# Sliding-window attention feeding four gated experts: q and k loaded as 18 tokens per partition row and turned with an output stride of 18, batch 0 loaded first, masks from four selects

## The chip, the core and the metric

The kernel runs on one core of a Trainium2 chip. The metric is the device time of one execution in microseconds (us). The compute engines are PE (TensorE, matmuls and weight loads), DVE (VectorE), ACT (ScalarE) and POOL (GpSimd). SP only issues DMAs, and "SPq" and "ACTq" are the places in the traces where SP and ACT issue them. A time such as "67.9" without more is a moment of the profiled execution, counted from the start of its span.

## The reference

Eight batches of eight heads, 576 tokens, 64 elements per head. Each token attends to the tokens at most 32 away; the heads' results, put side by side, are the 512-wide input of a mixture of four attention experts, of which each token uses two.

```
scores = 0.125 * q @ k^T ;  scores = where(|i - j| <= 32, scores, -1e9)
x = softmax(scores) @ v                       # [8, 8, 576, 64] -> [8, 576, 512]
logits = x @ w_gate ;  w = softmax over the two largest of four
for e in range(4):
    a = causal softmax(0.125 * (x @ wq[e]) @ (x @ wk[e])^T)
    out += [e chosen] * w_e * (a @ (x @ wv[e])) @ wo[e]
```

## The kernel before

The work is cut by batch, and each batch passes through three stages. W (window scores) makes the masked exponentials AT of one batch; M makes the window result, the gate and the experts' scores of the batch before it; Z makes the experts' output of the batch before that. The stages N, W, M and Z of one pass i belong to batches i+1, i, i-1 and i-2. The text `ORDER` writes out the steps of one pass, and the loop runs it for i = 0 to 9. Inside `tc.manual_schedule()` every engine executes its instructions in exactly that written order, and so does SP with its DMAs: an instruction that waits holds up all later ones of its engine. What stands ahead of that block is ordered by a scheduler.

For each batch b and group g of four heads, `load_qk` brings q and k into tiles `qn` and `kn` of 128 partitions by 18 blocks by 64 elements: partition 32*h+p holds the tokens p, p+32, p+64, ..., so each piece in memory is one token's 64 floats, 256 bytes. Four DMAs, one per head, fill a tile. `turn` (L199) transposes a tile on DVE in 32 by 32 blocks into `Tkn` or `Tqn`, which have the 64 elements on partitions and the 576 tokens in order along the row; two instructions per tile. `win_scores` multiplies them on PE (L220), ACT takes the exponential (L226) and POOL multiplies it with the mask `MASK` (L227).

`load_v` reads v in 256-byte pieces (L89, L91) and then makes a second, shifted copy inside the on-chip memory with two DMAs (L93, L94), for which SP waits until v has landed. `win_av` (L255) needs both copies, and `win_sums` (L234), `win_norm` (L270, L272) follow. The two DVE waits that matter below are the turns of `kn`: in pass i, "W turn 1 kn" stands behind `win_norm` and ahead of the cast of the experts' keys (`QKE`, L347); "N turn 0 kn" stands ahead of the cast of the rest of the experts' values (`VE`, L368), whose end frees a PSUM slot for the next `win_scores`.

SP's order in a later pass is: three output stores (L448, L450), q and k of group 0 of the next batch, v of the next batch, the two copies, q and k of group 1. `load_weights` issues all weights from ACT's queue at the start, and DVE casts them to bf16 before its first turn. The masks are built on POOL: `MASK` from 18 selects over pieces of 96 to 160 columns, `SEL` (a 0/1 matrix that spreads a head's sums over 64 rows) from three selects over 2,048 columns.

Of the kernel before, what the change touches and what calls it, by code (L numbers as in the profile page):

```python
# [21 lines left out]
S = 576  # L22
HS = 288
# [3 lines left out]
def kernel(  # L27
# [23 lines left out]
        return min(128, S - 128 * t)  # L51

    consts = ctx.enter_context(tc.tile_pool(name="consts", bufs=1))
    natp = ctx.enter_context(tc.tile_pool(name="natp", bufs=3))
    qkt = ctx.enter_context(tc.tile_pool(name="qkt", bufs=2))
    vp = ctx.enter_context(tc.tile_pool(name="vp", bufs=2))
# [18 lines left out]
    vsb = {}  # L75

    def load_qk(b, g):
        for nm, src in (("qn", q), ("kn", k)):
            t = natp.tile([128, 18, 64], F32, name=nm, tag=nm)
            for hh in range(4):  # L80
                nc.sync.dma_start(t[32 * hh:32 * hh + 32, :, :],  # L81
                                  src[b, 4 * g + hh].rearrange("(tb p) d -> p tb d", p=32))
            nat[nm, b, g] = t

    def load_v(b):
# [9 lines left out]
        vsb[b] = t  # L95

    load_qk(0, 0)
    load_v(0)
    load_qk(0, 1)


    ident = consts.tile([128, 128], F32, name="ident")
    make_identity(nc, ident)
    ident_bf = consts.tile([128, 128], BF16, name="ident_bf")
    nc.vector.tensor_copy(ident_bf, ident)


    MASK = consts.tile([128, S], F32, name="MASK")
    nc.vector.memset(MASK, 1.0)
    for par in range(2):  # L110
        for m in range(5 - par):
            lo, hi = 128 * m - 32 + 64 * par, 128 * m + 96 + 64 * par
            if par == 1 and m == 0:
                lo = 0
            if par == 1 and m == 3:
                hi = S
            c0 = max(0, lo)
            c1 = min(S, hi)
            key0 = 128 * m + 64 * par
            ap = MASK[64 * par:64 * par + 64, c0:c1]  # L120
            nc.gpsimd.affine_select(ap, ap, pattern=[[1, c1 - c0]], compare_op=IS_GE, fill=0.0,
                                    base=c0 - key0 + 32, channel_multiplier=-1)
            nc.gpsimd.affine_select(ap, ap, pattern=[[-1, c1 - c0]], compare_op=IS_GE, fill=0.0,
                                    base=key0 + 32 - c0, channel_multiplier=1)

    OH = consts.tile([128, 8, 32], F32, name="OH")
    nc.vector.memset(OH, 0.0)
# [12 lines left out]
    nc.vector.tensor_reduce(NM, nmt, axis=AXX, op=ADD)  # L140

    SEL = consts.tile([128, 4, 4, 128], BF16, name="SEL")
    nc.vector.memset(SEL, 0.0)
    selv = SEL[:, :, :, :].rearrange("p j a (h d) -> p j (a h) d", d=64)
    for r in range(3):
        nc.gpsimd.affine_select(selv, selv, pattern=[[-32, 4], [-1, 8], [0, 64]], compare_op=NEQ,
                                fill=1.0, base=-8 * r, channel_multiplier=1)

    SELG = consts.tile([128, 4], F32, name="SELG")
    nc.vector.memset(SELG, 0.0)  # L150
# [10 lines left out]
    WV = consts.tile([128, NDT, 256], BF16, name="WV")  # L161
    WO = consts.tile([128, 2, DM], BF16, name="WO")

    def load_weights():
        nc.scalar.dma_start(WG[:, :, 0:4], moe_w_gate.rearrange("(t p) e -> p t e", p=128))
        for j in range(2):
            for n, src in enumerate((moe_wq, moe_wk)):
                if n == 0:
                    tmp = yp.tile([128, 2, NDT, 128], F32, name="tmpw", tag="ysb")
                for eo in range(2):  # L170
                    nc.scalar.dma_start(tmp[:, n, :, 64 * eo:64 * eo + 64],
                                        src[2 * j + eo].rearrange("(t p) d -> p t d", p=128))
                nc.vector.tensor_copy(WQK[j][n], tmp[:, n, :, :])
        tmpv = yp.tile([128, NDT, 256], F32, name="tmpv", tag="ysb")
        for e in range(E):
            nc.scalar.dma_start(tmpv[:, :, 64 * e:64 * e + 64],
                                moe_wv[e].rearrange("(t p) d -> p t d", p=128))
        nc.vector.tensor_copy(WV, tmpv)
        tmpo = yp.tile([128, 2, DM], F32, name="tmpo", tag="ysb")
        for e in range(E):  # L180
            nc.scalar.dma_start(tmpo[64 * (e % 2):64 * (e % 2) + 64, e // 2, :], moe_wo[e])
        nc.vector.tensor_copy(WO, tmpo)

# [9 lines left out]
    def turn(b, g, nm):  # L195
        T = qkt.tile([128, 2, S], F32, name="T" + nm, tag="T" + nm)
        n_ = nat.pop((nm, b, g))
        for dh in range(2):
            nc.vector.transpose(T[:, dh, :].rearrange("p (t x) -> p t x", x=32),  # L199
                                n_[:, :, 32 * dh:32 * dh + 32])  # L200
        qt_[b, g, nm] = T

    def win_scores(b, g, half):
        QT, KT = qt_[b, g, "qn"], qt_[b, g, "kn"]
        if half == 0:
            AT[b, g] = atp.tile([128, 4, S], F32, name="AT", tag="AT")
        A = AT[b, g]
        sl = [slot("sc0"), slot("sc1")]
        c0 = HS * half
        eb, ob = EBLK[half], OBLK[half]  # L210
        for s in range(3):
            for dh in range(2):
                for par, blk in ((0, eb), (1, ob)):
                    if s >= len(blk):
                        continue
                    m, lo, hi = blk[s]
                    k0 = 128 * m + 64 * par
                    for hh in range(4):
                        r = slice(32 * hh, 32 * hh + 32)
                        nc.tensor.matmul(  # L220
                            sl[hh // 2][64 * par:64 * par + 64, hh % 2, lo - c0:hi - c0],
                            KT[r, dh, k0:k0 + 64], QT[r, dh, lo:hi],
                            start=(dh == 0), stop=(dh == 1), skip_group_check=True)
        for p in range(2):
            ap = A[:, 2 * p:2 * p + 2, c0:c0 + HS]
            nc.scalar.activation(ap, sl[p][:, :, 0:HS], EXP, scale=scale_att)  # L226
            nc.gpsimd.tensor_tensor(out=ap, in0=ap,  # L227
                                    in1=MASK[:, None, c0:c0 + HS].to_broadcast([128, 2, HS]), op=MULT)

    def win_sums(b):  # L230
        ss = slot1("sums")
# [202 lines left out]
    def moe_y(b, t0):  # L434
# [14 lines left out]
        else:  # L449
            nc.sync.dma_start(out[b, 512:576, :], ysb[0:64, 0, :])  # L450


    load_weights()

    ORDER = """
        M win_av 0 | M win_av 1 | M win_sums | M win_av 2 | M win_av 3 | Z moe_av 1
        M win_norm 0 | M win_norm 1 | Z moe_turn 0 | M win_norm 2 | M win_norm 3 | Z moe_turn 1
# [62 lines left out]
```

## Time and profile before

| | |
|---|---|
| median of 3 runs | 387.86 us (380.88, 387.86, 388.38) |
| the profiled execution | 382.31 us, its span 380.6 us |
| mean granted TensorE clock in it | 0.929 of full speed |
| PE busy | 280.9 us (74% of the span) |
| DVE busy | 162.6 us (43%) |
| POOL busy | 151.8 us (40%) |
| ACT busy | 144.9 us (38%) |
| DMA packets | 129,351, of which 120,848 under 512 bytes |

The span is the time from the first to the last instruction. "Chain that ended last" is the work followed back from the last instruction, each step to what released it. "Waits" lists who stood idle and what ended it. The timeline gives start and length of each instruction or run of like instructions, and in brackets the idle time in front of it with its releaser. In the windows, the clock is the one granted to TensorE as a share of its full 2.4 GHz (0.50 is its lower level of 1.2 GHz).

### The profile page before, as it was taken

The numbers are of one execution on the slowest core, as the hardware profiler recorded it, in microseconds if no ns is written. First come the engines' busy times: TensorE is split into PE (matmuls) and PEld (weight loads), VectorE is DVE, ScalarE is ACT, GpSimd is POOL, SyncE is SP. The second block draws the span as 40 slices with busy tenths as digits, with TensorE's granted clock in tenths as the row PEclk, the third lists the DMA queues.
The fourth block names the chain that finished last, engine by engine and source line by source line (L and its number), as shares of the span: only waits on it lengthen the run. The fifth ranks groups of instructions, "written<-read, shape, count | busy, mean of one in ns | idle before, by whom it ended". The sixth has DMA issues, their size and how long they took to land.

```text
span 380.6 us, 12750 instructions
## 1 busy us (share of the span) xinstructions
PE 280.9 (74%) x5680; PEld 207.7 (55%) x5680; DVE 162.6 (43%) x375; ACT 144.9 (38%) x217; POOL 151.8 (40%) x208
## 2 busy tenths in 40 slices
PE   0050686688897889869885879678978998798864
PEld 0040574457655665648564765566556856583641
DVE  4420441553726262444644282527443355343341
ACT  0120223254163615543363326361635245623432
POOL 8732336244252714443534425271436154612110
PEclk9999999689898996999899999999996989996986
DMA  9999969979089943969097918875597812002103
GB/s 164 201 158 184 183 137 174 171 153 122 2 198 178 159 67 117 185 143 157 14 231 156 180 23 199 178 152 76 165 186 143 107 49 79 3 4 87 39 0 124
DMA packets 129351, 48.02 MB, mean 126 GB/s; under 512 B 120848, under 2 KB 120848, under 8 KB 129296
## 3 DMA queue, kind: packets, MB, share of 16 engines
q1 hardware_dynamic: 122112, 45.10, 65.9%
q10 hardware_dynamic: 7184, 2.11, 3.4%
q8 instruction: 44, 0.72, 0.8%
q14 instruction: 11, 0.09, 0.1%
HBM read 30.42 MB, written 9.44 MB: 105 GB/s over the span
## 4 chain that ended last, share of the span: by engine, by line
PE 45%; DMA 14%; SPq 14%; DVE 11%; ACT 9%; issue 4%; ACTq 1%; POOL 0%; DVEq 0%; POOLq 0%
SPq L81 11%; PE sc L220 10%; PE u L255 10%; DMA kn<-in_k_dram 9%; PE po L408 7%; PE py L441 5%; ACT ATE L385 5%; PE sums L234 4%; DVE XTF L272 3%; PE pp L340 3%; ACT AT L226 2%; DVE Tkn L199 2%; PE pv L362 2%; PE ps L382 2%; DVE OE L417 2%
## 5 line engine op out<-in xcount | busy, mean ns | idle before, releaser
L227 POOL TENSOR_TENSOR AT<-AT,MASK 128x576 f32<-128x576 f32 x64 | 88.6, 1406 | 101.1 <-ACT AT L226 101.1
L220 PE MATMUL sc<-Tqn,Tkn 32*64 32x128 f32 (+3 forms) x2560 | 62.0, 311 | 56.6 <-DVE Tqn L199 35.4
L220 PEld LDWEIGHTS sc<-Tqn,Tkn 32*64 32x64 f32 x2560 | 52.0, 156 | 67.6 <-DVE Tqn L199 22.6
L226 ACT ACTIVATE AT<-sc 128x576 f32<-128x576 f32 x64 | 38.2, 648 | 120.1 <-PE sc L220 120.1
L385 ACT ACTIVATE ATE<-ps 128x1024 bf16<-128x1024 f32 x64 | 50.8, 835 | 27.7 <-PE ps L382 27.6
L274 POOL CAST XTB<-XTF 128x576 bf16<-128x576 f32 x32 | 21.3, 666 | 72.8 <-DVE XTF L272 72.8
L255 PE MATMUL u<-AT,vsb 128*64 128x64 f32 (+1 forms) x1024 | 39.0, 235 | 7.5 <-ACT ATE L385 6.8
L199 DVE STREAM_TRANSPOSE Tkn<-kn 128x576 f32<-128x576 f32 x32 | 22.9, 751 | 47.5 <-DMA kn<-in_k_dram 47.5
L255 PEld LDWEIGHTS u<-AT,vsb 128*64 128x64 f32 x1024 | 35.5, 142 | 10.7 <-ACT ATE L385 7.6
L259 ACT COPY us<-u 128x576 f32<-128x576 f32 x32 | 20.4, 638 | 39.3 <-PE u L255 39.3
L382 PE MATMUL ps<-QKE 64*128 64x512 bf16 (+2 forms) x192 | 22.7, 294 | 13.4 <-ACT AT L226 6.8
L389 POOL TENSOR_SCALAR_AFFINE_SELECT ATE<-ATE 128x384 bf16<-128x384 bf16 x32 | 15.9, 521 | 40.8 <-ACT ATE L385 40.8
L347 DVE CAST QKE<-pp 128x576 bf16<-128x576 f32 x16 | 12.0, 747 | 47.1 <-PE pp L340 47.1
L408 PE MATMUL po<-VE,ATE 128*128 128x65 bf16 (+2 forms) x480 | 27.9, 201 | 2.0 <-POOL ATE L389 1.6
L408 PEld LDWEIGHTS <-ATE 128*128 128x128 bf16 (+2 forms) x480 | 22.1, 103 | 8.1 <-POOL ATE L389 1.7
L415 DVE RECIPROCAL po<-po 128x8 f32<-128x8 f32 (+1 forms) x32 | 6.2, 194 | 47.1 <-PE po L408 46.5
L446 ACT COPY ysb<-py 128x1024 f32<-128x1024 f32 (+1 forms) x24 | 19.5, 880 | 17.6 <-PE py L441 9.2
L441 PE MATMUL py<-WO,OTT 128*128 128x512 bf16 (+1 forms) x80 | 25.3, 463 | 1.2 <-DVE OTT L432 1.1
L199 DVE STREAM_TRANSPOSE Tqn<-qn 128x576 f32<-128x576 f32 x32 | 22.8, 750 | 0.0
L272 DVE TENSOR_TENSOR XTF<-us,rb 128x576 f32<-128x576 f32 x32 | 22.3, 737 | 0.6 <-PE rb L270 0.6
L239 DVE RECIPROCAL sums<-sums 128x144 f32<-128x144 f32 x8 | 8.5, 1067 | 32.6 <-PE sums L234 32.6
L362 PE MATMUL pv<-WV,XTB 128*128 128x256 bf16 (+1 forms) x160 | 21.9, 289 | 0.0
(67 smaller groups left out, 317.3 us busy)
## 6 DMA issues: line engine op xcount, KB each, us to landing
qn<-in_q_dram SPq DMA_DIRECT2D x64, 144.0 KB, 5.3
kn<-in_k_dram SPq DMA_DIRECT2D x64, 144.0 KB, 5.3
vsb<-in_v_dram SPq DMA_DIRECT2D x32, 256.0 KB, 5.6
out_dram<-ysb SPq DMA_DIRECT2D x16, 512.0 KB, 2.9
vsb<-vsb SPq DMA_DIRECT2D x8, 512.0 KB, 5.1
vsb<-vsb SPq DMA_DIRECT2D x8, 384.0 KB, 7.6
vsb<-in_v_dram SPq DMA_DIRECT2D x8, 128.0 KB, 4.4
out_dram<-ysb SPq DMA_DIRECT2D x8, 128.0 KB, 3.4
```

The source lines that it names most:

```text
L81: nc.sync.dma_start(t[32 * hh:32 * hh + 32, :, :], src[b, 4 * g + hh].rearrange("(tb p) d -> p tb d", p=32))
L199: nc.vector.transpose(T[:, dh, :].rearrange("p (t x) -> p t x", x=32), n_[:, :, 32 * dh:32 * dh + 32])
L220: nc.tensor.matmul(sl[hh // 2][64 * par:64 * par + 64, hh % 2, lo - c0:hi - c0], KT[r, dh, k0:k0 + 64], QT[r, dh, lo:hi], start=(dh == 0), ...
L226: nc.scalar.activation(ap, sl[p][:, :, 0:HS], EXP, scale=scale_att)
L227: nc.gpsimd.tensor_tensor(out=ap, in0=ap, in1=MASK[:, None, c0:c0 + HS].to_broadcast([128, 2, HS]), op=MULT)
L255: nc.tensor.matmul(u[64 * x:64 * x + 64, half, lo - HS * half:hi - HS * half], V[:, c, h, :], A[:, h % 4, lo:hi], start=True, stop=True, s ...
L272: nc.vector.tensor_tensor(out=XTF[:, pair, :].rearrange("p (a c) -> p a c", c=HS), in0=st.pop(("us", b, pair)), in1=rb[:, :, 0:HS], op=MULT)
L362: nc.tensor.matmul(o, XTB[:, dt, 128 * t:128 * t + n], WV[:, dt, :], start=(dt == 0), stop=(dt == NDT - 1))
L382: nc.tensor.matmul(ps[0:rows, eo, at:at + hi - lo], QKE[r, 1, 128 * kt:128 * kt + nrow(kt)], QKE[r, 0, lo:hi], start=True, stop=True)
L385: nc.scalar.activation(ATE[0:rows, :, 512 * c:512 * c + w], ps[0:rows, :, 0:w], EXP, scale=scale_moe)
L408: nc.tensor.matmul(po[0:n, eo, 65 * qt:65 * qt + 65], ATE[0:nk, eo, o:o + n], VE[0:nk, kt, 2 * j + eo, :], start=(kt == 0), stop=(kt == qt))
L441: nc.tensor.matmul(py[0:n, t - t0, :], OTT[:, j, 128 * t:128 * t + n], WO[:, j, :], start=(j == 0), stop=(j == 1))
```

## The change

q and k tiles are loaded by one DMA each, in which partition 32*h+p holds the 18 consecutive tokens 18*p to 18*p+17: one piece of 4,608 bytes per partition. The tokens then lie across the blocks, and `turn` writes each block's 32 columns 18 floats apart to put them in order again. k is loaded before q. At the start both groups of batch 0 are loaded before its v; group 0 of batch 1 follows, then the weights, now from SP's queue and behind the copies of v. All four turns of batch 0 are done first; those of batch 1's group 0 stand ahead of the sums of batch 0. The weights' casts go from DVE at the start to ACT in pass 1. The window mask is built from four selects over 512 or 640 columns, `SEL` from three selects over 32 columns and one spreading copy on DVE. For batch 0 the masks are multiplied on DVE. One dummy exponential loads ACT's table early.

```diff
 def load_qk(b, g):
-        for nm, src in (("qn", q), ("kn", k)):
+        for nm, src in (("kn", k), ("qn", q)):
             t = natp.tile([128, 18, 64], F32, name=nm, tag=nm)
-            for hh in range(4):
-                nc.sync.dma_start(t[32 * hh:32 * hh + 32, :, :],
-                                  src[b, 4 * g + hh].rearrange("(tb p) d -> p tb d", p=32))
+            nc.sync.dma_start(t[:, :, :].rearrange("p s d -> p (s d)"),
+                              src[b, 4 * g:4 * g + 4].rearrange("h (p s) d -> (h p) (s d)", s=18))
...
     load_qk(0, 0)
+    load_qk(0, 1)
     load_v(0)
-    load_qk(0, 1)
...
+    MASKP = consts.tile([128, 640], F32, name="MASKP")
...
+        nc.gpsimd.affine_select(ap, ap, pattern=[[0, nb], [1, 128]], compare_op=IS_GE, fill=0.0,
+                                base=0, channel_multiplier=-1)
+        nc.gpsimd.affine_select(ap, ap, pattern=[[0, nb], [-1, 128]], compare_op=IS_GE, fill=0.0,
+                                base=64, channel_multiplier=1)
+    MASK = MASKP[:, 32:608]
...
+    def spread_sel(_):
+        nc.vector.tensor_copy(SEL[:, :, :, :].rearrange("p j a (h d) -> p (j a h) d", d=64),
+                              sels[:, :, :].rearrange("p j h -> p (j h)")[:, :, None].to_broadcast([128, 32, 64]))
...
-    def load_weights():
-        nc.scalar.dma_start(WG[:, :, 0:4], moe_w_gate.rearrange("(t p) e -> p t e", p=128))
+    def load_weights(_):
+        nc.sync.dma_start(WG[:, :, 0:4], moe_w_gate.rearrange("(t p) e -> p t e", p=128))
...
+    def cast_weights(_):
+        for j in range(2):
+            for n in range(2):
+                nc.scalar.copy(WQK[j][n], wtmp[j][:, n, :, :])
+        nc.scalar.copy(WV, wtmp["v"])
+        nc.scalar.copy(WO, wtmp["o"])
...
 def turn(b, g, nm):
         for dh in range(2):
-            nc.vector.transpose(T[:, dh, :].rearrange("p (t x) -> p t x", x=32),
+            nc.vector.transpose(T[:, dh, :].rearrange("p (t s) -> p s t", s=18),
                                 n_[:, :, 32 * dh:32 * dh + 32])
...
 def win_scores(b, g, half):
-            nc.gpsimd.tensor_tensor(out=ap, in0=ap,
-                                    in1=MASK[:, None, c0:c0 + HS].to_broadcast([128, 2, HS]), op=MULT)
+            eng = nc.vector if b == 0 else nc.gpsimd
+            eng.tensor_tensor(out=ap, in0=ap,
+                              in1=MASK[:, None, c0:c0 + HS].to_broadcast([128, 2, HS]), op=MULT)
...
+    early = {("turn", 0), ("turn", 1), ("load_qk", 1)}
     with tc.manual_schedule():
+        load_qk(1, 0)
+        load_weights(0)
         turn(0, 0, "kn")
         turn(0, 0, "qn")
+        turn(0, 1, "kn")
+        turn(0, 1, "qn")
+        spread_sel(0)
         for i in range(B + 2):
...
+                if i == 0 and (fn, b) in early and not (fn == "load_qk" and args == ["1"]):
+                    continue
+                if i == 1 and fn == "win_sums":
+                    turn(1, 0, "kn")
+                    turn(1, 0, "qn")
+                if fn == "win_norm" and i == 1 and args == ["0"]:
+                    cast_weights(0)
```

The order of SP's DMAs from the start up to the group 1 of batch 1 was this. The number in a tile's name tells two tiles apart: `kn_99` and `kn_117` are groups 0 and 1 of batch 0, `kn_307` and `kn_427` those of batch 1; the weights are not on this queue.

```order
L81 DMA qn_94<-in_q_dram 32x18x64 x4
L81 DMA kn_99<-in_k_dram 32x18x64 x4
L89 DMA vsb_104<-in_v_dram 128x8x64 x4
L91 DMA vsb_104<-in_v_dram 64x8x64
L93 DMA vsb_104<-vsb_104 64x4x512
L94 DMA vsb_104<-vsb_104 64x3x512
L81 DMA kn_117<-in_k_dram 32x18x64 x4
L81 DMA kn_307<-in_k_dram 32x18x64 x4
L89 DMA vsb_312<-in_v_dram 128x8x64 x4
L93 DMA vsb_312<-vsb_312 64x4x512
L81 DMA kn_427<-in_k_dram 32x18x64 x4
```

Of the changed kernel the same stretch reads as follows; here `kn_97` and `kn_101` are batch 0, `kn_201` and `kn_387` batch 1.

```order
L82 DMA kn_97<-in_k_dram 128x1152
L82 DMA kn_101<-in_k_dram 128x1152
L90 DMA vsb_105<-in_v_dram 128x8x64 x4
L82 DMA kn_201<-in_k_dram 128x1152
L94 DMA vsb_105<-vsb_105 64x4x512
L82 DMA qn_203<-in_q_dram 128x1152
L175 DMA tmpw_206<-in_moe_wq_dram 128x4x64 x2
L179 DMA tmpv_216<-in_moe_wv_dram 128x4x64 x4
L183 DMA tmpo_221<-in_moe_wo_dram 64x512 x4
L90 DMA vsb_286<-in_v_dram 128x8x64 x4
L94 DMA vsb_286<-vsb_286 64x4x512
L82 DMA kn_387<-in_k_dram 128x1152
```

Batch 0's second group now stands ahead of its v, and 17 weight DMAs stand between the first copies and batch 1's v; group 1 of batch 1 is still behind batch 1's copies.

On DVE the start, from the first turn to the end of the window's normalising in pass 1, has these turns in the kernel before (`Tkn_369` is batch 1's group 0, `Tkn_625` its group 1):

```order
L173 CAST WQ1_213<-tmpw_225 128x512
L178 CAST WV_215<-tmpv_232 128x1024
L199 STREAM_TRANSPOSE Tkn_246<-kn_99 128x576 x2
L199 STREAM_TRANSPOSE Tkn_252<-kn_117 128x576 x2
L199 STREAM_TRANSPOSE Tkn_369<-kn_307 128x576 x2
L239 RECIPROCAL sums_516<-sums_516 128x144
L272 TENSOR_TENSOR XTF_595<-us_495,rb_597 128x576
L199 STREAM_TRANSPOSE Tkn_625<-kn_427 128x576 x2
L347 CAST QKE_703<-pp_714 128x576
```

and these in the changed one:

```order
L207 STREAM_TRANSPOSE Tkn_226<-kn_97 128x18x32 x2
L207 STREAM_TRANSPOSE Tqn_235<-qn_103 128x18x32 x2
L148 COPY SEL_163<-sels_164 128x2048
L236 TENSOR_TENSOR AT_239<-AT_239,MASKP_122 128x2x288 x4
L236 TENSOR_TENSOR AT_340<-AT_340,MASKP_122 128x2x288 x4
L207 STREAM_TRANSPOSE Tkn_475<-kn_201 128x18x32 x2
L248 RECIPROCAL sums_481<-sums_481 128x144
L281 TENSOR_TENSOR XTF_566<-us_454,rb_568 128x576
L207 STREAM_TRANSPOSE Tkn_596<-kn_387 128x18x32 x2
L356 CAST QKE_668<-pp_679 128x576
```

The casts of the weights have gone, eight mask multiplications have come, and the turn of batch 1's group 1 still stands ahead of the cast of the experts' keys.

## Rows read from the trace of the kernel before

**Rows 1.** The page: span, and the chain that ended last, by line
```profile
span 380.6 us, 12750 instructions
...
SPq L81 11%; PE sc L220 10%; PE u L255 10%; DMA kn<-in_k_dram 9%; PE po L408 7%; PE py L441 5%; ACT ATE L385 5%; PE sums L234 4%; DVE XTF L272 3%; PE pp L340 3%; ACT AT L226 2%; DVE Tkn L199 2%; PE pv L362 2%; PE ps L382 2%; DVE OE L417 2%
```

**Rows 2.** The page's DMA queues and issues: size of each, median us to landing
```profile
q10 hardware_dynamic: 7184, 2.11, 3.4%
...
kn<-in_k_dram SPq DMA_DIRECT2D x64, 144.0 KB, 5.3
...
vsb<-vsb SPq DMA_DIRECT2D x8, 384.0 KB, 7.6
```

**Rows 3.** Waits of 0 to 88.8 us: who waited, total us, times, longest us
```profile
DVE Tkn L199 <- DMA kn<-in_k_dram: 32.5, 4, 16.1
...
PE ps L382 <- DVE QKE L347: 4.9, 1, 4.9
```

**Rows 4.** Waits of 88.8 to 294.7 us, the five batches with loads
```profile
DVE Tkn L199 <- DMA kn<-in_k_dram: 15.0, 5, 3.5
...
PE sc L220 <- DVE VE L368: 11.5, 5, 2.8
```

**Rows 5.** Timeline 0 to 75 us: start, length, engine, what, idle before it
```profile
22.03 2.74 PE L220 MATMUL sc<-Tqn,Tkn 32*64 32x96 f32 x84 [22.03 <-DVE Tqn L199]
...
46.36 4.18 PE L255 MATMUL u<-AT,vsb 128*64 128x96 f32 x64
...
57.99 1.34 PE L220 MATMUL sc<-Tqn,Tkn 32*64 32x96 f32 x73 [0.28 <-DVE XTF L272]
...
63.72 1.39 PE L220 MATMUL sc<-Tqn,Tkn 32*64 32x64 f32 x80
...
67.89 1.44 DVE L199 STREAM_TRANSPOSE Tkn<-kn 128x576 f32<-128x576 f32 x2 [9.29 <-DMA kn<-in_k_dram]
...
70.02 0.61 PE L382 MATMUL ps<-QKE 64*128 64x512 bf16 x2 [4.91 <-DVE QKE L347]
```

**Rows 6.** Timeline 130 to 173 us, one batch of the steady part
```profile
156.82 1.23 DVE L365 CAST VE<-pv 128x1024 bf16<-128x1024 f32 x1 [2.18 <-PE pv L362]
...
159.51 0.18 DVE L317 SCALAR_TENSOR_TENSOR pl<-MSK,pl 128x20 f32<-128x20 f32 x1
...
161.81 0.38 PE L220 MATMUL sc<-Tqn,Tkn 32*64 32x96 f32 x4
...
162.36 1.44 DVE L199 STREAM_TRANSPOSE Tkn<-kn 128x576 f32<-128x576 f32 x2 [2.67 <-DMA kn<-in_k_dram]
...
164.16 1.37 PE L220 MATMUL sc<-Tqn,Tkn 32*64 32x96 f32 x76 [1.97 <-DVE VE L368]
```

**Rows 7.** Windows: us, busy per engine (count), PE clock, DMA share, GB/s
```profile
0.00:2.00 2.00, 0.00 (x0) 0.00 (x0) 0.85 (x3) 0.00 (x0) 1.11 (x8) 1.00 0.04 10
0.00:20.00 20.00, 0.00 (x0) 0.00 (x0) 8.09 (x16) 1.28 (x1) 15.70 (x40) 1.00 1.18 184
36.00:38.00 2.00, 0.00 (x0) 0.00 (x0) 0.00 (x0) 0.00 (x0) 0.00 (x0) 1.00 1.41 169
108.00:110.00 2.00, 2.00 (x47) 1.49 (x49) 0.30 (x1) 1.00 (x2) 0.00 (x0) 1.00 1.02 367
```

**Rows 8.** Groups by line and shape on DVE: busy us, mean ns of one
```profile
L199 DVE STREAM_TRANSPOSE Tkn<-kn 128x576 f32<-128x576 f32 x32 | 22.9, 751 | 47.5 <-DMA kn<-in_k_dram 47.5
...
L272 DVE TENSOR_TENSOR XTF<-us,rb 128x576 f32<-128x576 f32 x32 | 22.3, 737 | 0.6 <-PE rb L270 0.6
...
L328 DVE TENSOR_TENSOR G<-pl,ssum 128x20 f32<-128x20 f32 x8 | 1.6, 194 | 0.3
...
L309 DVE TENSOR_TENSOR GE<-pl,m 128x20 f32<-128x20 f32 x8 | 1.4, 178 | 0.3
```

**Rows 9.** Groups by line and shape on ACT
```profile
L446 ACT COPY ysb<-py 128x1024 f32<-128x1024 f32 x16 | 15.8, 1025 | 17.6 <-PE py L441 9.2 <-issue 7.7 <-ACT AT L226 0.6
L345 ACT CAST QKE<-pp 128x576 bf16<-128x576 f32 x16 | 10.2, 638 | 13.0 <-issue 7.8 <-PE pp L340 5.2
```

More of the change, by code (lines that the diff above doesn't have):

```diff
@@ L53 @@
     consts = ctx.enter_context(tc.tile_pool(name="consts", bufs=1))
+    stage = ctx.enter_context(tc.tile_pool(name="stage", bufs=1))
     natp = ctx.enter_context(tc.tile_pool(name="natp", bufs=3))
@@ L97 @@
     load_qk(0, 0)
+    load_qk(0, 1)
     load_v(0)
-    load_qk(0, 1)
     ident = consts.tile([128, 128], F32, name="ident")
     make_identity(nc, ident)
+    warm = consts.tile([128, 1], F32, name="warm")
+    nc.scalar.activation(warm, ident[:, 0:1], EXP)
     ident_bf = consts.tile([128, 128], BF16, name="ident_bf")
     nc.vector.tensor_copy(ident_bf, ident)
[L108 to L124, printed above, removed]
+    MASKP = consts.tile([128, 640], F32, name="MASKP")
+    nc.vector.memset(MASKP[0:64, :], 1.0)
+    nc.vector.memset(MASKP[64:128, :], 0.0)
+    nc.vector.memset(MASKP[64:128, 64:576], 1.0)
+    for p0, ap in ((0, MASKP[0:64, :]), (64, MASKP[64:128, 64:576])):
+        ap = ap.rearrange("p (m c) -> p m c", c=128)
+        nb = 5 if p0 == 0 else 4
+        nc.gpsimd.affine_select(ap, ap, pattern=[[0, nb], [1, 128]], compare_op=IS_GE, fill=0.0,
[3 more added lines that the diff above has]
+    MASK = MASKP[:, 32:608]
     OH = consts.tile([128, 8, 32], F32, name="OH")
@@ L142 @@
     SEL = consts.tile([128, 4, 4, 128], BF16, name="SEL")
-    nc.vector.memset(SEL, 0.0)
-    selv = SEL[:, :, :, :].rearrange("p j a (h d) -> p j (a h) d", d=64)
+    sels = consts.tile([128, 4, 8], BF16, name="sels")
+    nc.vector.memset(sels, 0.0)
     for r in range(3):
-        nc.gpsimd.affine_select(selv, selv, pattern=[[-32, 4], [-1, 8], [0, 64]], compare_op=NEQ,
-                                fill=1.0, base=-8 * r, channel_multiplier=1)
+        nc.gpsimd.affine_select(sels, sels, pattern=[[-32, 4], [-1, 8]], compare_op=NEQ, fill=1.0,
+                                base=-8 * r, channel_multiplier=1)
+    def spread_sel(_):
+        nc.vector.tensor_copy(SEL[:, :, :, :].rearrange("p j a (h d) -> p (j a h) d", d=64),
+                              sels[:, :, :].rearrange("p j h -> p (j h)")[:, :, None].to_broadcast([128, 32, 64]))
     SELG = consts.tile([128, 4], F32, name="SELG")
@@ L450, in moe_y @@
             nc.sync.dma_start(out[b, 512:576, :], ysb[0:64, 0, :])
-    load_weights()
     ORDER = """
```

21 lines of the change are left out of this document (9 added, 12 removed).

## Prediction

> **What bounds the kernel now.** I read the chain that ended last first. No engine fills it: its largest entry by line is SP issuing q and k (SPq L81, 11% of a span of 380.6 us), and another 9% is the landing of `kn` [rows 1]. The waits then tell where the lateness costs something. Up to 88.8 us DVE stands idle 32.5 us in four waits for `kn`, the longest 16.1; the last of them stops PE for 4.9 us, because the cast of the experts' keys stands behind the turn [rows 3]. In the five later batches that have loads, DVE waits 15.0 us for `kn` and PE loses 11.5 us of it behind the `VE` cast [rows 4]. So the loads of q and k cost time twice: once in the start-up, once a little in each batch. The reader is to see in the timeline that PE had nothing else to do: in one batch the turn starts at 162.36 after 2.67 us of idling, and PE, done with its few ready matmuls at 161.81 + 0.38 = 162.19, goes on only at 164.16 [rows 6].
>
> **The later batches.** There the stores go first on SP, then q and k of the next batch. Eight issues become two, and 256-byte pieces become 4,608-byte ones. A tile is four DMAs of 144.0 KB, 590 kB [rows 2]. In 256-byte pieces q and k move at 169 GB/s, and the two-microsecond window in which output stores of 2 KB rows dominate shows 367 GB/s [rows 7]. The trace has no piece of 4,608 bytes, so the price of a tile lies between 590/367 = 1.6 us and 590/169 = 3.5 us; I take 2.0 us (about 300 GB/s), near the row it is most like. At either end `kn` lands well before DVE asks, since seven issues ahead of it fall away as well. DVE is then free at 159.51 + 0.18 = 159.69; the two transposes (1.44) and the small `VE` cast (about 0.4) end at 161.5, ahead of PE's 162.19. All 11.5 us of PE's waits would go, were the transposes unchanged.
>
> **The strided write.** The transposes now write each run of 32 elements 72 bytes apart. No transpose in the trace writes with a stride. What bounds it: 751 ns for 576 elements is about one element per cycle of 1.04 ns plus 0.15 us, which is the lower end (+0). The nearest row with a strided write is `G`, 20 elements written 20 bytes apart: 194 ns, against 178 ns for `GE`, the same count written in order [rows 8], so 0.8 ns per element. For 576 elements that is +0.46 us; rounding up to one whole extra cycle gives +0.6 us, which I take, since 20 elements are a thin sample. The Trainium skill (SBUF — State Buffer, section "Door 1: The DMA port swizzle") speaks against the change here: accesses need at least two hits on a 16-byte line for full bandwidth, and each crossing to a new line pays; it gives no size for DVE. The `G` row agrees in direction. Without any penalty the sum below would be 4 us lower; its harsh reading is a rival.
>
> At +1.2 us per turn, most turns have cover: the turn of `qn` in pass i ends 2.18 us before DVE is needed for the large `VE` cast [rows 6]. The turn at 159.69 then ends the `VE` cast at 162.7, 0.5 us after PE's 162.19, so five batches lose 5 x 0.5 = 2.5 us plus a little semaphore time. Gain of the later batches: 11.5 - 2.8 = **8.7 us**.
>
> **The start-up.** What PE waits for at 67.89 is `kn` of batch 1, group 1 [rows 5]. I follow SP's new order up to it. Transfers begin at about 2.0 (the first two microseconds move 10 GB/s) [rows 7]. Four tiles of batch 0 at 2.0: 10.0. Then v, 4 x 256 + 128 KB = 1.18 MB, still in 256-byte pieces at 169 GB/s, 7.0 us: 17.0, known to SP at about 17.7. `kn` of batch 1 runs meanwhile. The copies of v take 7.6 us from issue [rows 2]: 25.3. `qn` of batch 1: 27.3. The weights are 2.11 MB [rows 2]: 0.52 MB of 2 KB rows at 367 and 1.58 MB at 169, 10.8 us: 38.1. v of batch 1, 7.0 us: 45.1, known at 45.8. Its copies: 53.4. `kn` of group 1 behind them, 2.0: **55.4**, where it was 67.89: 12.5 us earlier. Its own strided turn takes 1.2 back and stands directly ahead of the cast that PE waits for: 11.3 us. Bounds: at 1.6 us a tile, and with the copies not holding up `kn`, it lands at about 51; at 3.5 us a tile at about 64.
>
> What else the edit moves must be done before that. `win_av` of batch 0 starts when the copies land, 25.3 instead of 46.36 [rows 5]. Its scores need `qn` (6.7, with its turn 9.4) and four times 2.74 us [rows 5], about 21 with the exponentials. The masks on DVE: four turns end near 13.4, the spreading copy of 2,048 columns costs 2.6 us at the pace of `XTF` (737 ns for 576), and eight products at 737 ns end near 22; the copies of v cover that up to 25.3. The mask selects on POOL (15.70 us busy of the first 20 [rows 7]) are shorter and needed at 16, so I put them at nothing. From `win_av` to the first scores of batch 1 took 57.99 - 46.36 = 11.6 us: 36.9. The casts now in ACT's way cost four times 638 ns and twice 1025 ns [rows 9], 4.6 us: 41.5, later than the weights' landing. From there to the point where PE has nothing left took 65.11 - 57.99 = 7.1 us [rows 5]: 48.6. So the casts lie under the wait for `kn` with 7 us to spare, and without that wait they would cost their 4.6 us.
>
> **The sum.** 382.31 us for the profiled execution (its span 380.6 and 1.7 around it), less 11.3 at the start, less 8.7 in the later batches: 362.3, so **362 us**. The median of the three runs is 387.86, 1.5% above the profiled one, and the lowest is 380.88; if the changed kernel scatters alike, its median may lie up to 5 us above the sum, which the range takes in.
>
> **Rivals.**
> *Strided writes are dear (the other side).* At c cycles per element a transpose costs 0.15 + 0.6c us. At c = 4 (2.55 us) `kn` of group 1 is turned 3.6 us later than unstrided; in each batch the `qn` turn eats its 2.18 us of slack and 1.4 us more, and the turn at 159.69, itself 1.4 later, ends the cast at about 166.6 instead of 164.1: 2.5 us lost in each of five batches, 1.5 in the sixth. 382.3 - 12.5 + 3.6 + 14 = 387, no change; at c = 5 the same working gives about 400. It becomes slower by 2% (390) from about 4.3 cycles. The `G` row, under two cycles, speaks against it. The Trainium skill's rule on lines (SBUF — State Buffer, the same section) leaves the size open. The turns would read 2.5 us and more each. Slower 0.04, unchanged 0.05.
> *The loads do not speed up per byte* (3.5 us a tile). `kn` lands at 64, 3.5 us earlier, 1.2 of it lost in the turn; the later batches still gain 8.7, since seven fewer issues and one tile ahead instead of two are enough. 371 us. The 367 GB/s row speaks against it. 0.11.
> *`kn` of group 1 comes before PE needs it*, because weights and copies overlap better than my queue in single file. Then 48.6 is the floor: 70.02 - 48.6 = 21.4 instead of 11.3, and the sum is 352. For it: DMA shares above 1 in the windows mean that transfers overlap [rows 7]; against it: SP still waits for v before issuing the copies, and `kn` is behind them. 0.18.
> *Another wait takes the place in the later batches*, for example the keys' or the values' cast further back on DVE, and only the start-up gains: 371 us. Against it: PE's other waits on DVE do not hang on the loads. 0.10.
>
> **How the numbers follow.** My forecast has 0.52, with 355 to 369 as its own range. The cases with 371 and 352 add 0.39, and the overall range of 350 to 376 takes them in, with their scatter. About 2% is what a measurement of this kernel can tell from no change. Faster by over 2% needs less than about 375 on the profiled scale, which the forecast and three rivals give: 0.91 by the cases, cut to 0.86 for a cost that I have not seen; within 2%: 0.09; slower: 0.05.
>
> **What would show it.** Right: transposes of about 1.35 us; DVE's waits for `kn` after the start gone, and PE's wait behind the `VE` cast under 1 us per batch; the last wait for `kn` ending near 55, with PE stopped before it; `win_av` of batch 0 near 25. Wrong: transposes above 2.5 us; `kn` still awaited in each batch; or `win_av` of batch 0 not starting before 35, which would mean that v or its copies are later than the sum has them.

## The result, and the profile after

The median is 349.82 us (347.33 to 353.33) against 386.77 for the kernel before beside it: ratio 0.910, 95% interval 0.895 to 0.925. The forecast was 362 with a range of 350 to 376, so the direction was right, and the time lies 0.2 us below the range: the gain was larger than forecast. The profiled execution took 351.94 us, 30.4 less than the 382.31 before, where 20.0 were forecast. Medians here and below are over all executions, while ratios and intervals leave out those in a slower state at a lower granted clock; of the kernel before, 27 executions beside the experiments took 375.86 to 392.84 us at mean clocks of 0.958 to 0.897.

The page of the kernel after, span and chain that ended last, by engine and by line:

```profile
span 350.2 us, 12556 instructions
...
PE 62%; DVE 15%; ACT 9%; DMA 5%; SPq 4%; issue 3%; ACTq 0%; POOL 0%; POOLq 0%; DVEq 0%
PE sc L228 13%; PE u L264 9%; PE pp L349 8%; PE po L417 7%; PE py L450 7%; ACT ATE L394 5%; PE pv L371 5%; PE sums L243 4%; DVE XTF L281 4%; ACT AT L234 4%; DVE Tkn L207 3%; DMA kn<-in_k_dram 3%; PE pl L308 3%; PE ps L391 3%; PE pg L299 2%
```

SP's issuing of q and k, the largest entry before at 11% [rows 1], is gone from the list; the landing of `kn` fell from 9% to 3%, and PE now fills 62% of the chain.

I cut both profiles at the first `win_av` of pass 2 (88.80 before, 73.16 after) and at that of pass 7 (294.65 and 261.69). Timeline of the kernel after, the places of [rows 5]:

```profile
23.01 3.79 PE L264 MATMUL u<-AT,vsb 128*64 128x64 f32 x60 [1.84 <-DMA vsb<-vsb]
...
49.83 2.34 DVE L207 STREAM_TRANSPOSE Tkn<-kn 128x576 f32<-128x576 f32 x2 [14.65 <-DMA kn<-in_k_dram]
...
52.80 0.61 PE L391 MATMUL ps<-QKE 64*128 64x512 bf16 x2 [12.37 <-DVE QKE L356]
...
73.16 2.06 PE L264 MATMUL u<-AT,vsb 128*64 128x96 f32 x58 [0.97 <-ACT ATE L394]
```

The last awaited `kn` is turned at 49.83 instead of 67.89, PE goes on at 52.80 instead of 70.02, and pass 2 begins **15.6 us** earlier. The waits of 73.2 to 261.7 us, the five later batches (us in total, times, longest):

```profile
DVE VE L374 <- PE pv L371: 4.7, 5, 0.9
...
PE pp L349 <- ACT ATE L394: 2.1, 5, 0.4
PE ps L391 <- ACT AT L234: 2.0, 5, 0.4
PE pv L371 <- ACT AT L234: 2.0, 5, 0.4
...
PEld sc L228 <- DVE VE L377: 1.2, 5, 0.2
```

DVE's 15.0 us for `kn` and PE's 11.5 behind `VE` [rows 4] are no longer among them. Windows of the same five batches, first before, then after; the columns are the length, busy time (instructions) of PE, weight loads, DVE, ACT and POOL, then PE clock, DMA share and GB/s:

```profile
88.80:294.65 205.85, 169.53 (x3551) 126.58 (x3551) 96.48 (x226) 89.37 (x136) 85.39 (x106) 0.94 0.74 137
```

```profile
73.16:261.69 188.53, 163.50 (x3546) 123.55 (x3551) 113.22 (x226) 89.01 (x136) 85.34 (x106) 0.97 0.54 146
```

They are **17.3 us** shorter. PE's work is the same, but it was busy 6.0 us less, at a mean clock of 0.97 instead of 0.94. What follows pass 7 took 88.5 instead of 85.95 us, **2.6** more. The sum, -15.6 - 17.3 + 2.6, is -30.3.

The turns and the other new work of DVE (groups by line and shape: busy us, mean ns of one):

```profile
L207 DVE STREAM_TRANSPOSE Tkn<-kn 128x576 f32<-128x576 f32 x32 | 37.3, 1240 | 15.4 <-DMA kn<-in_k_dram 15.4
...
L236 DVE TENSOR_TENSOR AT<-AT,MASKP 128x576 f32<-128x576 f32 x8 | 5.6, 755 | 2.7 <-ACT AT L234 2.7
L148 DVE COPY SEL<-sels 128x2048 bf16<-128x2048 bf16 x1 | 1.2, 1214 | 0.0
```

### The profile page after: what moved, and what is told of

It is laid out like the page before. It is cut to its first block, busy times and chain, and to the rows that moved or that the text cites. A ratio compares the mean times of both kernels' runs of the same rounds, so it can differ in the third digit from the quotient of the medians.

```text
span 350.2 us, 12556 instructions
## 1 busy us (share of the span) xinstructions
PE 279.6 (80%) x5672; PEld 206.9 (59%) x5680; DVE 190.4 (54%) x380; ACT 148.6 (42%) x224; POOL 131.9 (38%) x186
## 4 chain that ended last, share of the span: by engine, by line
PE 62%; DVE 15%; ACT 9%; DMA 5%; SPq 4%; issue 3%; ACTq 0%; POOL 0%; POOLq 0%; DVEq 0%
PE sc L228 13%; PE u L264 9%; PE pp L349 8%; PE po L417 7%; PE py L450 7%; ACT ATE L394 5%; PE pv L371 5%; PE sums L243 4%; DVE XTF L281 4%; ACT AT L234 4%; DVE Tkn L207 3%; DMA kn<-in_k_dram 3%; PE pl L308 3%; PE ps L391 3%; PE pg L299 2%
## 5 line engine op out<-in xcount | busy, mean ns | idle before, releaser
L236 POOL TENSOR_TENSOR AT<-AT,MASKP 128x576 f32<-128x576 f32 x56 | 77.8, 1411 | 65.0 <-ACT AT L234 65.0
L228 PE MATMUL sc<-Tqn,Tkn 32*64 32x128 f32 (+3 forms) x2560 | 60.2, 302 | 19.0 <-DVE Tqn L207 8.3
L228 PEld LDWEIGHTS sc<-Tqn,Tkn 32*64 32x64 f32 x2560 | 50.4, 150 | 29.6 <-DVE Tqn L207 8.8
L394 ACT ACTIVATE ATE<-ps 128x1024 bf16<-128x1024 f32 x64 | 51.0, 836 | 36.1 <-PE ps L391 35.9
L207 DVE STREAM_TRANSPOSE Tkn<-kn 128x576 f32<-128x576 f32 x32 | 37.3, 1240 | 15.4 <-DMA kn<-in_k_dram 15.4
L268 ACT COPY us<-u 128x576 f32<-128x576 f32 x32 | 20.5, 639 | 41.0 <-PE u L264 41.0
L207 DVE STREAM_TRANSPOSE Tqn<-qn 128x576 f32<-128x576 f32 x32 | 37.2, 1240 | 0.0
L417 PE MATMUL po<-VE,ATE 128*128 128x65 bf16 (+2 forms) x480 | 27.1, 198 | 2.0 <-POOL ATE L398 1.6
L450 PE MATMUL py<-WO,OTT 128*128 128x512 bf16 (+1 forms) x72 | 24.1, 461 | 3.2 <-DVE OTT L441 2.0
L391 PEld LDWEIGHTS <-QKE 64*128 64x128 bf16 x192 | 7.0, 96 | 27.0 <-DVE QKE L356 15.1
```

The source lines that it names most:

```text
L207: nc.vector.transpose(T[:, dh, :].rearrange("p (t s) -> p s t", s=18), n_[:, :, 32 * dh:32 * dh + 32])
L228: nc.tensor.matmul(sl[hh // 2][64 * par:64 * par + 64, hh % 2, lo - c0:hi - c0], KT[r, dh, k0:k0 + 64], QT[r, dh, lo:hi], start=(dh == 0), ...
L236: eng.tensor_tensor(out=ap, in0=ap, in1=MASK[:, None, c0:c0 + HS].to_broadcast([128, 2, HS]), op=MULT)
L391: nc.tensor.matmul(ps[0:rows, eo, at:at + hi - lo], QKE[r, 1, 128 * kt:128 * kt + nrow(kt)], QKE[r, 0, lo:hi], start=True, stop=True)
L394: nc.scalar.activation(ATE[0:rows, :, 512 * c:512 * c + w], ps[0:rows, :, 0:w], EXP, scale=scale_moe)
L417: nc.tensor.matmul(po[0:n, eo, 65 * qt:65 * qt + 65], ATE[0:nk, eo, o:o + n], VE[0:nk, kt, 2 * j + eo, :], start=(kt == 0), stop=(kt == qt))
```

## The experiments

Two places had to be explained: the start (15.6 us, forecast 11.3) and the later batches (17.3, forecast 8.7).

**The loads and turns alone.** The kernel before with these three edits of the change and none of its others:

```diff
-        for nm, src in (("qn", q), ("kn", k)):
+        for nm, src in (("kn", k), ("qn", q)):
...
-            for hh in range(4):
-                nc.sync.dma_start(t[32 * hh:32 * hh + 32, :, :],
-                                  src[b, 4 * g + hh].rearrange("(tb p) d -> p tb d", p=32))
+            nc.sync.dma_start(t[:, :, :].rearrange("p s d -> p (s d)"),
+                              src[b, 4 * g:4 * g + 4].rearrange("h (p s) d -> (h p) (s d)", s=18))
...
-            nc.vector.transpose(T[:, dh, :].rearrange("p (t x) -> p t x", x=32),
+            nc.vector.transpose(T[:, dh, :].rearrange("p (t s) -> p s t", s=18),
```

> The kernel before with only the loads of 4,608-byte pieces (k first) and the strided turns; order at the start, masks and casts as before. Theory 'bytes ahead': what counts at the start is how many microseconds of transfers stand ahead of k of batch 1, group 1, and these are the same bytes in either order; that tile lands at 48 to 53 us as in the changed kernel (49.8), and the time is 348 to 356 us, ratio to before 0.90 to 0.92. Rival 'start order': loading batch 0 first and the weights later makes a good part of the start's 15.6 us; then this kernel stays at 358 us or more, ratio 0.925 or more.

346.97 us, ratio 0.913 (0.901 to 0.924), beside 0.910 for the whole change. Pass 2 begins at 70.25. So the loads and turns carry the whole gain; batch 0 first, the casts on ACT and the new masks add nothing to it that can be measured. At the start PE waits 23.1 us for `Tqn` here, where after has 8.3, but `kn` of batch 1 is there when it is asked for.

**The new start alone.** The change with the old loads and turns (k first, as in the change):

> The changed kernel with the old loads (four DMAs per tile in 256-byte pieces, but k first) and the old turns; its start order, masks and casts are kept. Theory 'bytes ahead': k of batch 1, group 1 lands at 62 to 66 us, so the start gains 2 to 5 us at most. In the later batches k now goes out four issues earlier, about 3 us, which is as long as DVE waited there (15.0 us in five batches); if the order of k and q is enough, DVE's waits for k there fall under 4 us in total and the time is 366 to 372 us; if the size of the pieces is needed, they stay above 8 us and the time is 375 to 383 us. Rival 'start order': the start alone gives 8 us or more, 360 to 366 us.

384.50 us, ratio 1.010 (1.004 to 1.016). `kn` of batch 1, group 1 was turned from 64.67, as expected, and DVE's wait for it in the later batches was 0.3 us instead of 15.0; yet a later batch still took 41.0 us (205.0 for five). Neither theory had that: the wait was gone and its cost was not.

**k ahead of q alone**, the kernel before with one line changed:

```diff
-        for nm, src in (("qn", q), ("kn", k)):
+        for nm, src in (("kn", k), ("qn", q)):
```

> The kernel before with one edit: k is loaded ahead of q. Theory, after the start-alone kernel: DVE's wait for k in the later batches falls from 15.0 us to under 3, and still the time falls by less than 4 us against the kernel before, since PE runs more of it at the low clock: mean clock 0.88 to 0.92, time 380 to 387 us. Rival 'the wait is the price': 11 us of the later batches and 3 us of the start are gained, 368 to 373 us.

384.16 us, ratio 1.015 (1.002 to 1.029), as the first theory had it: the same riddle with one line. No wait for `kn` in the later batches, and they took 210.4 us, 4.6 more than before. Its waits there (84.5 to 294.9 us) show new names (`ps` are the experts' scores, `pp` the projections of their queries and keys, `ATE` their exponentials):

```profile
PE ps L382 <- ACT AT L226: 5.7, 10, 0.7
PE pp L340 <- ACT QKE L345: 3.9, 5, 0.8
...
PE ps L382 <- ACT ATE L385: 2.8, 5, 0.6
```

**Turns that write in order**, the change with the turn of before:

```diff
-            nc.vector.transpose(T[:, dh, :].rearrange("p (t s) -> p s t", s=18),
+            nc.vector.transpose(T[:, dh, :].rearrange("p (t x) -> p t x", x=32),
```

> The changed kernel with turns that write in order (stride 1 instead of 18 floats); the reordering of the tokens is left out, so scores belong to permuted tokens; all else is the same. Theory: each transpose falls from 1.24 back to 0.75 us; of the 32 us that this saves DVE only what stands on PE's path is gained, 0.4 us in each of five later batches and 1 us at the start: 346 to 349 us against 350. Rival 'DVE is the bound by now': DVE is 54% busy, and 5 us or more are gained, 345 us or less.

348.00 us, ratio 0.911 (after: 0.910). The 0.49 us more per transpose, 31 us of DVE in all, cost nothing that the time can tell; in the profile the five later batches are 186.0 us instead of 188.5, about the 2 us that the theory gave them.

**Four DMAs a tile**, in pieces of 4,608 bytes:

```diff
-            nc.sync.dma_start(t[:, :, :].rearrange("p s d -> p (s d)"),
-                              src[b, 4 * g:4 * g + 4].rearrange("h (p s) d -> (h p) (s d)", s=18))
+            for hh in range(4):
+                nc.sync.dma_start(t[32 * hh:32 * hh + 32, :, :].rearrange("p s d -> p (s d)"),
+                                  src[b, 4 * g + hh].rearrange("(p s) d -> p (s d)", s=18))
```

> The changed kernel with four DMAs per tile again (one per head), each of 32 partitions by one piece of 4,608 bytes: the piece stays large, the number of issues is the old one. Theory 'size of the piece': q and k land at most 2 us later per batch, ahead of DVE's need, and the time stays within 3 us of the changed kernel, 346 to 353 us. Rival 'number of issues': SP's issue time is what the change saved; k of batch 1, group 1 comes 5 us later and DVE waits for k again in the later batches, 360 us or more.

354.93 us, ratio 0.940 (0.933 to 0.948), between the two theories. The later batches are those of after (187.8 us); the start is later (pass 2 at 79.63). It is not SP's issuing that costs this: SP issued a tile's four DMAs in 1.8 us, but the tiles moved more slowly, with the DMA engines as full as before. Below are the windows of 4 to 8 us, in which hardly anything but tiles of q and k moves: in after, in this kernel (with SP's first four issues), and in the new start alone, whose loads differ from this kernel's by their 256-byte pieces.

```profile
4.00:8.00 4.00, 0.00 (x0) 0.00 (x0) 3.41 (x4) 0.00 (x0) 3.80 (x15) 1.00 1.01 405
```

```profile
4.00:8.00 4.00, 0.00 (x0) 0.00 (x0) 2.59 (x3) 0.00 (x0) 3.80 (x15) 1.00 1.02 232
...
0.80 1.79 SPq L83 DMA_DIRECT2D kn<-in_k_dram  x4
```

```profile
4.00:8.00 4.00, 0.00 (x0) 0.00 (x0) 0.26 (x1) 0.00 (x0) 3.80 (x15) 1.00 1.39 169
```

Larger pieces bring 169 to 232 GB/s; the step from 232 to 405 comes with one DMA over 128 partitions in place of four over 32, at the same piece size. Whether it is the count of DMAs or the partitions that each one reaches was not tried apart.

**`kn` of batch 1, group 1, earlier**: its load behind the weights, ahead of v of batch 1.

```diff
         load_weights(0)
+        load_qk(1, 1)
         turn(0, 0, "kn")
...
-                if i == 0 and (fn, b) in early and not (fn == "load_qk" and args == ["1"]):
+                if i == 0 and (fn, b) in early:
```

> The changed kernel with q and k of batch 1, group 1 issued right behind the weights, ahead of batch 1's v. Theory: PE's stop from 40.4 to 52.8 us goes but for 1 or 2 us, since the tile then lands at about 39; the low clock of 44 to 65 us, which follows that stop, goes too or shrinks below 8 us; the time is 331 to 338 us, ratio 0.855 to 0.875. Rival 'the next wait': the values or another tile are late next, PE stops elsewhere for 8 us or more, 342 us or more.

346.08 us, ratio 0.913: the stop of 12.4 us went, but the time hardly fell, as the rival had it. Timeline around the new stop:

```profile
52.05 2.34 DVE L207 STREAM_TRANSPOSE Tkn<-kn 128x576 f32<-128x576 f32 x2 [7.22 <-DMA kn<-in_k_dram]
...
54.69 2.30 PE L228 MATMUL sc<-Tqn,Tkn 32*64 32x96 f32 x76 [7.36 <-DVE VE L377]
```

The next tile, batch 2's group 0, is behind v and its copies now. **Both tiles ahead of v** was the answer:

```diff
         load_weights(0)
+        load_qk(1, 1)
+        load_qk(2, 0)
         turn(0, 0, "kn")
...
+                if i == 1 and fn == "load_qk" and args == ["0"]:
+                    continue
```

> The changed kernel with q and k of batch 1, group 1 and of batch 2, group 0 issued right behind the weights, ahead of batch 1's v. In the kernel that moved only the first of these, PE stopped 7.4 us for the second instead. Theory: both stops go, the long low clock of the start goes with them, the first value product of pass 2 starts at 54 to 60 us (73.2 in the changed kernel, 65.0 with one tile moved), and the time is 331 to 339 us. Rival: v of batch 1, now later, or another wait stops PE by 7 us or more, 343 us or more.

**333.04 us**, ratio 0.882 (0.869 to 0.895), pass 2 at 58.33: as expected, and it beats both kernels. SP's order alone, at the same transfer speed, was worth another 17 us.

**Doubled traffic.** After, with a second copy of all the q and k loads of a pass in the old form, read by nobody:

```diff
+    def load_dummy(b):
+        for g in range(2):
+            for src in (k, q):
+                t = dump.tile([128, 18, 64], F32, name="dump", tag="dump")
+                for hh in range(4):
+                    nc.sync.dma_start(t[32 * hh:32 * hh + 32, :, :],
+                                      src[b, 4 * g + hh].rearrange("(tb p) d -> p tb d", p=32))
...
+                    if i > 0 and fn == "load_qk" and args == ["1"]:
+                        load_dummy(b)
```

> The changed kernel with additional loads that nobody reads: in each pass from 1 on, behind q and k of group 1, the same q and k once more in 256-byte pieces (16 DMAs, 2.36 MB) into scratch tiles, while the DMA engines are otherwise idle. Theory 'small pieces lower the clock': the traffic itself goes with more time at the low clock of TensorE, as in the two kernels with 256-byte loads; the mean clock falls to 0.88 to 0.91, the later batches take 39.5 to 41 us instead of 37.7 and the time is 358 us or more, without new waits. Rival 'not the traffic': clock and batches stay as in the changed kernel, 347 to 354 us.

359.68 us, ratio 0.954 (0.939 to 0.970). By the median the first theory holds, but the four executions spread from 353.39 to 361.46, on both sides of its 358, and the profiled one, the fastest, does not show a lower clock in the later batches. Its window and one of its waits there:

```profile
69.74:261.94 192.20, 163.08 (x3545) 122.87 (x3550) 113.21 (x226) 88.85 (x136) 85.20 (x106) 0.98 0.94 203
```

```profile
PE u L273 <- issue: 3.4, 3, 2.2
```

With a DMA share of 0.94 (0.54 in after), PE waited up to 2.2 us for nothing that the profile shows. As a test of the theory it is undecided.

**The PSUM buffers.** What remained was the riddle of the small waits. The 288 large PSUM tiles share three buffers, and which one a tile takes is decided when the kernel is built. Between the builds PE's instructions stand in the same order (but for a few rows at the start), yet the buffers are dealt otherwise. In a steady batch, this many tiles back is the one whose buffer is taken over (3 is strict turn; `pg` is the gate, `sc` the window's scores, `pv` the experts' values):

```
tile                    pg pp pp sc sc ps pv ps ps pv ps pp pp sc sc
before                   3  3  3  3  3  2  4  3  3  3  3  3  2  2  5
k ahead of q alone       3  3  3  3  3  2  4  3  3  2  2  1  1  7  5
after, loads alone       3  3  3  3  3  3  3  3  3  3  3  3  2  2  5
```

In the second row a `pp` takes over the buffer of the `pp` just ahead of it, so PE waits for the cast out of it (`pp` <- ACT QKE). The new start with old loads has that same row. In four kernels I wrote the deal out, with one buffer per tag:

```diff
-    psum = ctx.enter_context(tc.tile_pool(name="psum", bufs=3, space=bass.MemoryType.PSUM))
+    psum = ctx.enter_context(tc.tile_pool(name="psum", bufs=1, space=bass.MemoryType.PSUM))
...
-        return psum.tile([128, 2, 512], F32, name=name, tag="PS")
+        return psum.tile([128, 2, 512], F32, name=name, tag="PS" + next(DEAL))
```

k ahead of q, old loads, the deal of "loads alone":

> The kernel before with k loaded ahead of q (256-byte loads as before), and the order in which its 288 large PSUM tiles take the three buffers written out as the build with the new loads and nothing else (e1_layout) has it. TensorE's instructions stand in the same order in all these builds; what differs is whose buffer a tile takes over, and so whom its first matmul waits for. Without the fixed order (e7_kfirst) time was 384.2, a batch 40.3 to 43.5 us, and TensorE waited 7.3 us for ACT AT and 5.4 us for ACT QKE. Theory 'buffers': that was the buffers; with the better order these two waits fall to 2 to 3 us and 0, the later batches to 37 to 39 us, the first win_av of pass 2 stays at 83 to 89 us, time 360 to 369. Rival 'small pieces': 256-byte traffic beside TensorE slows it whatever the buffers; the waits fall, but batches stay above 40 us and time at 377 to 387.

**362.55 us**, ratio 0.953 (0.940 to 0.966), against 384.16 and 1.015 with its own deal. Its five later batches:

```profile
84.91:273.18 188.27, 162.83 (x3550) 122.73 (x3550) 96.97 (x226) 88.86 (x136) 85.11 (x106) 0.97 0.80 149
```

188.3 us, the 188.5 of after, with 256-byte loads. So the new loads are worth nothing in the later batches once `kn` is in time and the deal is that of after. The rival, small pieces slowing PE, falls.

The loads alone, with the deal of "k ahead of q alone":

> e1_layout (new loads, k first, turns with a stride) with the PSUM buffers taken over in the order that e7_kfirst had. Theory 'buffers': the waits for ACT AT (7 us) and ACT QKE (5 us) come back beside 4,608-byte loads, the later batches go from 37.9 to 40.5 to 43 us, time 360 to 370 against 347 for e1_layout. Rival 'small pieces': the time comes from the loads, 345 to 352.

372.54 us, ratio 0.986 (0.977 to 0.996), some 26 us above the loads alone and a little beyond what was expected. Window of the five batches, and waits of the same stretch:

```profile
75.60:285.62 210.02, 176.29 (x3550) 130.75 (x3550) 113.73 (x226) 90.21 (x136) 85.32 (x106) 0.90 0.49 133
```

```profile
PE ps L387 <- ACT AT L231: 5.6, 10, 0.7
PE pp L345 <- ACT QKE L350: 3.9, 5, 0.8
...
PE ps L387 <- ACT ATE L390: 2.8, 5, 0.6
```

The waits are those of "k ahead of q alone", to 0.1 us. They add some 8 us, and PE is busy 12 us longer than in the loads alone (164.06) at a clock of 0.90: together about the 20.6 us by which the five batches grew.

The loads alone, with the deal of before:

> e1_layout with the PSUM buffers taken over in the order that the kernel before had (ps takes the buffer that the scores two tiles earlier held, and waits for their exp). Theory 'buffers': TensorE's wait for ACT AT on ps goes from under 3 to 5 us, a batch from 37.9 to between 38.5 and 40, time 351 to 359. Rival 'small pieces': 345 to 350.

350.42 us, ratio 0.920 (0.904 to 0.935) against 0.913 (0.901 to 0.924): the two are not told apart. With the new loads, the deal of before costs at most a few us.

The kernel before with the better deal:

> The kernel before, q first and 256-byte loads as they were, with only the PSUM buffers taken over in the order of e1_layout. Theory 'buffers': TensorE's wait for ACT AT (ps) falls from 5.3 us to 2 or 3, while VectorE's wait for kn (15.0 us) and TensorE's for VE (11.5 us) stay in the five later batches; these fall from 41.2 to between 39 and 40.5 us, time 372 to 381. Rival 'small pieces': no gain, 381 to 390. If time is under 370, the waits for kn cost nothing and the buffers were the whole of the later batches.

388.77 us, ratio 1.030 (1.025 to 1.035). The time lies in the rival's range, but the rival had no gain and not a loss, and its cause fell with the kernel that has k first. The waits in the five later batches:

```profile
DVE Tkn L205 <- DMA kn<-in_k_dram: 17.7, 5, 4.0
PE sc L226 <- DVE VE L374: 14.2, 5, 3.3
```

They took 213.1 us, with PE busy 176.0. With this deal, q first costs 26 us more than k first (388.77 against 362.55). The wait behind `VE` is 2.7 us longer than before (14.2 instead of 11.5), and PE's waits for `AT` are 2.0 shorter (1.3 us in `ps` and 2.0 in `pv` instead of 5.3), as if one stop had mostly moved into the other. Why PE is also busy 6.5 us longer than before stays open.

## Why the prediction was right, and where it was short

**The start: right in its place, 4.3 us short.** PE stopped before `kn` of batch 1, group 1, as forecast. The floor under it lay at 40.4 (52.80 - 12.37), not at 48.6: `win_av` of batch 0 ran in the main from 23.01 instead of 25.3, and the casts, put in PE's way with 4.6 us, ran on ACT from 32.0 to 36.1 beside PE's normalising and scores. This moved nothing, since PE waited for `kn` in any case. The term that was mis-sized is the transfer. A tile was put at 2.0 us, about 300 GB/s; in the kernel after:

```profile
4.00:6.00 2.00, 0.00 (x0) 0.00 (x0) 1.41 (x2) 0.00 (x0) 1.80 (x4) 1.00 1.02 403
```

At 403 GB/s it is 1.46 us, below the lower bound of 1.6. The forecast put the speed down to the pieces alone; "four DMAs a tile" shows that pieces of 4,608 bytes in DMAs over 32 partitions stop at 232 GB/s, about 2.5 us a tile. That 2.0 came so near is in part luck, since the DMA over 128 partitions was not in the working. The six tiles in my chain give 3.2 us. `kn` was turned from 49.83, where 55.4 was forecast: 5.6 us early. The other 2.4 lie between that `win_av` and the copies of batch 1's v, which SP issued at 40.89 where 45.8 was forecast:

```profile
40.89 0.64 SPq L94 DMA_DIRECT2D vsb<-vsb  x1
```

This stretch, with `qn`, the weights and that v, took 17.9 us instead of 20.5. The strided turn took 0.9 back (2.34 against 1.44), and the way from the stop to pass 2 grew from 18.8 to 20.4 us, with a mean clock of 0.70 in it instead of 0.81. The low clock lay here:

```profile
44.50:65.00 20.50, 12.20 (x58) 7.76 (x58) 10.03 (x16) 4.06 (x6) 1.60 (x4) 0.50 0.90 238
```

This is the lower level, 1.2 GHz, entered after PE had stood still from 40.4. With 256-byte loads, k ahead of q and the deal of after, pass 2 begins at 84.9; the loads alone have it at 70.25. So the form of the loads is worth 14.7 us, nearly the whole 15.6. In the order of after the pieces and the DMAs can be read apart: pass 2 begins at 88.38 with the old loads (and their own deal), at 79.63 with 4,608-byte pieces in four DMAs, and at 73.16 with one DMA a tile.

One sum of the forecast is wrong without a result: four turns of 2.7 us in a row from 4.7 on end at 15.5, not near 13.4 (they ended at 13.5, since tiles and turns were faster). The products on DVE would still have ended before 25.3.

**The later batches: the wait right, a term missing.** Of PE's 11.5 us behind `VE`, 8.7 were to go. In a batch of after, the scores that wait for nothing take 1.39 us, and those behind the `VE` cast 1.80 (timeline):

```profile
130.77 1.39 PE L228 MATMUL sc<-Tqn,Tkn 32*64 32x64 f32 x80
...
139.81 1.80 PE L228 MATMUL sc<-Tqn,Tkn 32*64 32x96 f32 x80
```

So about 0.4 a batch, 2.0 in all, stays: 9.5 gone, near the forecast. The step that failed is the sum's silence on the clock. PE's busy time fell by 6.0 us though 2.0 of hidden waiting came into it: 8 us that the forecast had at nothing. At the low clock the same eight matmuls of after took 1.8 times as long (the first row is at clock 1.00, the second at 0.50):

```profile
36.98 1.16 PE L349 MATMUL pp<-XTB,WQ 128*128 128x288 bf16 x8
...
61.36 2.10 PE L349 MATMUL pp<-XTB,WQ 128*128 128x288 bf16 x8
```

Read in windows of half a microsecond, the low clock in the five batches went from 23.8 to 10.2 us; half of the difference, 6.8 us, is my estimate of its share in the 8. Both profiles are of one execution each, and with clocks of 0.958 to 0.897 among the executions of the kernel before these 8 us carry a scatter of several. The runs with other deals show that the busy time goes with PE's stops, whatever makes them: PE's busy time in the five batches is 161 to 165 us in all kernels without the wait for `kn` and without the bad deal (256-byte loads among them), and 172 to 177 in those with that deal or with the wait beside the better deal; before has 169.5. Another 1.3 us are the waits for `AT`, 4.0 in `ps` and `pv` after and 5.3 in `ps` before, the deal's share:

```profile
PE ps L382 <- ACT AT L226: 5.3, 10, 0.7
```

**The cause put to it was half right.** "Seven issues ahead of it fall away" was more than was needed: 256-byte loads with k first, four issues fewer ahead of it, have no wait either. What the prediction did not look at is that another form of load changes how the build deals out PSUM. The change had luck there: k ahead of q in the old form gets a deal that eats the gain, and with the new loads it does not. Whether the new loads with q first would still wait was not tried.

**The transposes: right.** 1.24 us against 1.35 taken; the `G` row's 0.8 ns per element gave 751 + 460 = 1.21. The Trainium skill's warning (SBUF — State Buffer, section "Door 1: The DMA port swizzle") agrees in direction, +0.49 us. The harsh reading, 2.5 us and more, fell, and writing in order gained nothing that the time can tell.

**What was put at nothing.** Masks, casts and the products on DVE (755 ns each) lay under other work, as said; the spreading copy took 1.2 us, where 2.6 was taken. Not forecast: the end, 2.6 us longer, with 22.1 us of low clock there instead of 19.9; the rest of it I did not follow up.

**The rivals.** "`kn` before PE needs it" (352) has the time nearest to the result, but not by its mechanism: PE still waited 12.4 us for `kn`. Removing that stop alone, in the experiment, turned up the next one; the rival's 352 would have needed both tiles early, and then the time was 333. The two cases with 371 fell: the tiles moved at over 400 GB/s, and no wait of the old one's size took its place in the later batches.

## What to carry to other kernels

Here a PE that stopped briefly in every batch paid twice, once in the wait and once in work at the lower clock: 9.5 us of waits went and some 8 us of PE's busy time with them. When an edit removes a wait and the time stands still, look at who waits for which PSUM buffer, since the form of a load can change the deal without a line of code or an instruction of PE moving; writing the deal out makes it part of the experiment. When loads get faster, test the size of the pieces and the form of the DMA one by one: here each brought about half of the start's gain. And follow the queue past the first tile that is late, because the next one stands behind the same transfers.

## What the chip showed that I had not expected

Tiles in 4,608-byte pieces moved at 405 GB/s with one DMA over 128 partitions and at 232 with four over 32 partitions each, against 169 with four in 256-byte pieces; the DMA share was at or above 1 in all three. A 32 by 32 transpose that writes 72 bytes apart took 1,240 ns for 576 columns, 0.85 ns per element more than in order. About 8 us of sub-microsecond waits in five batches, the longest 0.8 us, came with 12 us more of PE's busy time, at a clock of 0.90 instead of 0.97. And beside 203 GB/s of traffic PE waited up to 2.2 us for nothing that the profile shows.
